# Attention inside a stream of big products: four pieces a tile, or two shared with the neighbour

## The chip, the core and the metric

The kernel runs on one core of one Trainium2 chip. The core has a matrix engine, TensorE (PE in the profile, and PEld for its weight loads), and three others with instruction streams of their own: VectorE (DVE), ScalarE (ACT) and GpSimd (POOL). SyncE (SP) issues the transfers (DMA) between the device memory and the on-chip memory SBUF. PE writes its results to PSUM, eight banks of 512 float32 values for each of 128 partitions, from where DVE and ACT fetch them. The metric is the device time of one execution in microseconds; lower is better.

## The reference

Attention within chunks of 64 tokens, for 4 sequences of 576 tokens and 8 heads of width 64, followed by two feed-forward layers on the 2304 tokens of width 512, each with 2048 hidden units, all in float32:

```python
scores = scale * np.matmul(q_c, k_c.transpose(0, 1, 2, 4, 3))   # 64 x 64 per chunk and head
scores = scores - np.max(scores, axis=-1, keepdims=True)
attn = np.exp(scores)
attn = attn / (np.sum(attn, axis=-1, keepdims=True) + 1e-09)
x = np.matmul(attn, v_c)                                        # then 2304 tokens x 512
h = x @ w_in;  x = (h * sigmoid(1.702 * h)) @ w_out             # first layer
h = x @ w_in;  return (h * tanh(softplus(h))) @ w_out           # second layer, weights of its own
```

## The kernel before

The tokens are cut into 18 tiles of 128 and into NB = 6 blocks of three tiles, 384 tokens. A product of the feed-forward layers is computed to nearly full float32 accuracy from three reduced-precision matmuls: each operand is split into a high part and a low part, and `mm3` (lines 353 to 356) adds high x high, high x low and low x high.

The first layer runs in steps n = 0 to NA - 1 = 95, KF = 16 for each block (the loop at line 748). A step issues `in_proj` (line 358), 12 matmuls of 128 x 384 that give one slice h of 128 hidden units for the block, and, two steps late, `out_a` (line 384), 12 matmuls that add an earlier slice into the block's output, which stays in four banks, acc0 and acc1. Between them, ACT applies the activation (`gelu`, line 370), and DVE splits the result into gh and gl (lines 374 to 380). The slices h take turns in a ring of two banks (tag "h", pool `ps`): a new slice waits until the activation of the one two back has read its bank.

The attention of the next block runs between the steps of the present one, a tile every five steps, in four pieces. Each piece of PE work stands ahead of the `in_proj` of its step:

- step f = 1, 6, 11 of a block: `transposes` (line 253), eight transposes of q and k, which ACT and DVE then copy to SBUF (`take`, line 260);
- the step after: `scores` (line 266), 16 matmuls of 64 x 64 x 64 on quarters of the array; then on DVE the maximum and its subtraction (`shift`), on ACT the exponential, on DVE sums, reciprocal and `normalize`;
- two steps later: `attn_t` (line 311), four transposes of the attention weights, copied by ACT (`take_a`, line 317);
- the step after that: `pv` (line 322), 16 matmuls of 64 x 64 x 64 with v, whose result x is split into a high part by ACT (`x_hi`, line 338) and a low part by DVE (`x_lo`, line 348).

All four pieces of a tile write one PSUM buffer of two banks, tag "at", one after another (`psum`, line 242). The three tiles of the first block come before the loop, in an order that is written out (`PLAN`, line 24), where the buffers of acc0 and acc1 serve as well.

From the second block on, `second.step(n - KF)` (line 489) prepares the second layer's weights at the end of a step, in groups of eight steps (k = 0 to 7): `load` on SP, `scale` on ACT, `join` on DVE, then differences of halves, splits, and stores to device memory. Nothing in the first layer waits for these. The order on every engine is the order of the program: each engine takes its instructions one after another, and the semaphores between them are set when the program is built. The second layer (from line 826) begins after step 95.

Of the kernel before, what the change touches and what calls it, by code (L numbers as in the profile page):

```python
# [16 lines left out]
P = 128  # L17
CH = 64
# [17 lines left out]
def tile_kernel(  # L36
# [193 lines left out]
    class Attention:  # L230
# [16 lines left out]

        def load(self):
            self.q = load_tok(at, "q", q, self.i)
            self.k = load_tok(at, "k", k, self.i)  # L250
            self.v = load_tok(at, "v", v, self.i)

# [12 lines left out]

        def scores(self):
            self.pt = pt = self.psum("sc")
            for u in range(NP // 2):
                for c in range(2):
                    o = (u * 2 + c) * CH  # L270
                    for w in range(2):
                        c0 = (2 * u + w) * P + c * CH
                        for r in range(2):
                            rs = slice(r * CH, (r + 1) * CH)
                            nc.tensor.matmul(  # L275
                                pt[w * CH : (w + 1) * CH, r, o : o + CH],
                                self.qt[rs, c0 : c0 + CH],
                                self.kt[rs, c0 : c0 + CH],
                                start=True,
                                stop=True,  # L280
                            )
# [28 lines left out]

        def attn_t(self):
            self.pt = self.psum("at")
            for p in range(NP):
                s = slice(p * P, (p + 1) * P)
                nc.tensor.transpose(self.pt[:, 0, s], self.e[:, s], ident)  # L315

        def take_a(self, copy):
            if self.a is None:
                self.a = at.tile([P, DM], F32, tag="k", name=f"a{self.i}")
            copy(self.a, self.pt[:, 0, :])  # L320

        def pv(self):
            self.pt = pt = self.psum("pv")
            for p in range(NP):
# [13 lines left out]
        def x_hi(self, copy):  # L338
# [4 lines left out]
            sl = slice(self.t * P, (self.t + 1) * P)  # L343
            self.x = self.pt[:, :, 0 : NP * CH].rearrange("p c (a t) -> p c a t", a=NP)
            self.xo = [x[j][:, :, sl].rearrange("p a (c t) -> p c a t", c=2) for x in (xh, xl)]
# [61 lines left out]
    class Second:  # L407
# [81 lines left out]
        def step(self, s):  # L489
# [14 lines left out]
            if k == 0:  # L504
                self.scale(b)
                self.join(a)
            elif k == 1:
                self.load(c)
                self.join(b)
# [107 lines left out]
    with tc.manual_schedule():  # L617
# [79 lines left out]
        for step in PLAN.split():  # L697
            steps[step[0]](int(step[1:] or 0))
        att = tiles[TT]
        nxt, done, late_lo = tiles[TT + 1], 2, []  # L700

# [46 lines left out]
        for n in range(4, NA):  # L748
            f = n % KF

            if n < NA - KF and f > 0:
                at_step = (f - 1) % 5
                if at_step == 0:
                    att.transposes()
                    att.take("q", act)
                    att.take("k", act if n < KF else vec)
                    if att.i + 1 < NB * TT:
                        nxt = Attention(att.i + 1, usual)
                        nxt.load()
                elif at_step == 1:  # L760
                    att.scores()
                    att.shift()
                    att.exp()
                    att.sums()
                    att.normalize(nc.vector)
                elif at_step == 3:
                    att.attn_t()
                    att.take_a(act)
                elif at_step == 4:
                    att.pv()  # L770
                    att.x_hi(act)
                    att.x_lo()
                    att = nxt

# [329 lines left out]
```

## Time and profile before

| | |
|---|---|
| median of 3 runs | 841.75 us (841.61 to 842.65) |
| the profiled execution | 841.22 us, of which the span of the trace is 839.4 us |
| granted TensorE clock, mean | 0.998 of full speed |
| PE busy | 822.7 us |
| DVE busy | 550.8 us |
| ACT busy | 395.3 us |
| transfers | 180.31 MB, mean 215 GB/s |

Busy time is an average over stages with different limits, so it is read by stage. The first block's attention and its 16 steps take the first 100 us or so, the steps of the other blocks end at about 480 us, and the last attention piece stands at 401 us. PE's matmuls are pipelined: one starts every 0.17 us and is shown for 0.34 us, so what a stretch of PE costs is read from starts, not from busy time. A matmul in float32 on a quarter of the array leaves two records in the trace, so 16 of them are x32.

### The profile page before, as it was taken

What the parts mean: (1) busy time and instruction counts of PE and PEld (TensorE: products, weight loads), DVE (VectorE), ACT (ScalarE), POOL (GpSimd) and SP (SyncE); (2) the same over time, 40 slices, a digit from 0 to 9 for tenths busy, and PEclk for the clock granted to TensorE, in tenths of its full rate; (3) what the DMA queues carried; (4) which work ended last, traced back from release to release, by engine and by line L of the source; (5) the groups of instructions that cost most, each with busy time, mean ns of one, the idle gap of its engine ahead of it and who ended that gap; (6) DMA issues with size and microseconds to landing.
All of it is one profiled execution on the core that took longest, in us unless ns stands there. A gap on an engine that the chain in (4) does not pass through costs nothing.

```text
span 839.4 us, 15656 instructions
## 1 busy us (share of the span) xinstructions
PE 822.7 (98%) x6228; PEld 803.6 (96%) x6228; DVE 550.8 (66%) x1058; ACT 395.3 (47%) x711; POOL 0.7 (0%) x6
## 2 busy tenths in 40 slices
PE   6899999999999999999999999999999999999998
PEld 4799999999999999999999999999999999999997
DVE  6799757657676666766625466688565787565754
ACT  3899644445554544554312443356333465333542
POOL 0000000000000000000000000000000000000000
PEclk9999999999999999999999999999999999999999
DMA  9968635647667673854455178688788787877751
GB/s 242 280 190 246 173 114 150 202 159 242 177 197 212 184 213 138 264 151 164 161 179 226 60 253 322 232 288 261 256 300 282 260 276 260 269 253 240 262 199 57
DMA packets 120135, 180.31 MB, mean 215 GB/s; under 512 B 61440, under 2 KB 82432, under 8 KB 120064
## 3 DMA queue, kind: packets, MB, share of 16 engines
q1 hardware_dynamic: 120064, 179.33, 66.9%
q8 instruction: 49, 0.80, 0.4%
q14 instruction: 22, 0.18, 0.1%
HBM read 140.51 MB, written 38.80 MB: 214 GB/s over the span
## 4 chain that ended last, share of the span: by engine, by line
PE 89%; DVE 5%; ACT 2%; DMA 2%; issue 0%; SPq 0%; DVEq 0%
PE sum_acc L887 16%; PE sum_y L857 12%; PE h L857 9%; PE h L354 7%; PE acc L355 7%; PE acc L356 7%; PE acc L354 7%; PE h L355 7%; PE h L356 7%; PE sum_y L887 6%; DVE raw L201 1%; PE tr L258 1%; DMA raw<-in_moe_w_in_dram 1%; PE sc L275 1%; PE pv L330 1%; PE at L315 1%
## 5 line engine op out<-in xcount | busy, mean ns | idle before, releaser
L354 PE MATMUL h<-xh,wi 128*128 128x384 f32 x384 | 134.9, 351 | 0.0
L356 PE MATMUL h<-xh,wi 128*128 128x384 f32 x384 | 129.1, 336 | 1.7 <-DVE wi L163 1.7
L355 PE MATMUL acc<-gl,wo 128*128 128x384 f32 x384 | 129.2, 337 | 0.7 <-DVE gl L380 0.5
L355 PE MATMUL h<-xl,wi 128*128 128x384 f32 x384 | 129.2, 336 | 0.7 <-DVE xl L350 0.7
L356 PE MATMUL acc<-gh,wo 128*128 128x384 f32 x384 | 129.1, 336 | 0.0
L354 PE MATMUL acc<-gh,wo 128*128 128x384 f32 x384 | 129.0, 336 | 0.0
L372 ACT ACTIVATE t<-h 128x384 f32<-128x384 f32 x96 | 47.0, 489 | 125.4 <-PE h L356 100.0
L376 DVE CAST gh<-t 128x384 fp32r<-128x384 f32 x80 | 28.8, 360 | 90.5 <-ACT t L372 90.4
L354 PEld LDWEIGHTS h<-xh,wi 128*128 128x128 f32 x384 | 72.2, 188 | 2.0
L356 PEld LDWEIGHTS h<-xh,wi 128*128 128x128 f32 x384 | 72.2, 188 | 2.0 <-DVE wi L163 2.0
L355 PEld LDWEIGHTS acc<-gl,wo 128*128 128x128 f32 x384 | 72.2, 188 | 1.3 <-DVE gl L380 1.3
L355 PEld LDWEIGHTS h<-xl,wi 128*128 128x128 f32 x384 | 72.4, 188 | 0.9 <-DVE xl L350 0.9
L356 PEld LDWEIGHTS acc<-gh,wo 128*128 128x128 f32 x384 | 72.2, 188 | 0.0
L354 PEld LDWEIGHTS acc<-gh,wo 128*128 128x128 f32 x384 | 72.2, 188 | 0.0
L380 DVE TENSOR_TENSOR gl<-t,gh 128x384 fp32r<-128x384 f32 x96 | 53.5, 558 | 5.4 <-ACT gh L376 2.7
L867 ACT ACTIVATE v<-h 128x384 f32<-128x384 f32 x24 | 11.9, 494 | 61.9 <-PE h L857 61.9
L926 DVE TENSOR_TENSOR g_a<-u,sum_y 128x384 f32<-128x384 f32 x24 | 13.3, 554 | 32.5 <-PE sum_y L857 32.5
L926 DVE TENSOR_TENSOR v<-u,sum_y 128x384 f32<-128x384 f32 x24 | 13.3, 554 | 30.8 <-PE sum_y L857 30.8
L867 ACT ACTIVATE g_a<-g_a 128x384 f32<-128x384 f32 x24 | 12.6, 526 | 39.0 <-DVE g_a L926 39.0
L867 ACT ACTIVATE v<-v 128x384 f32<-128x384 f32 x24 | 12.6, 524 | 34.4 <-DVE v L926 34.4
L926 DVE TENSOR_TENSOR g_s<-v,g_s 128x384 f32<-128x384 f32 x48 | 26.8, 558 | 0.8
L887 PE MATMUL sum_acc<-fb_p,gh2p 128*128 128x256 f32 x144 | 26.3, 284 | 1.0 <-DVE c L926 1.0
(499 smaller groups left out, 1830.7 us busy)
## 6 DMA issues: line engine op xcount, KB each, us to landing
fs<-w_sums SPq DMA_DIRECT2D x84, 512.0 KB, 4.6
fb_p<-w_out_sums SPq DMA_DIRECT2D x60, 512.0 KB, 4.5
w_sums<-s SPq DMA_DIRECT2D x24, 512.0 KB, 2.7
fa<-w_outs SPq DMA_DIRECT2D x24, 512.0 KB, 4.5
raw<-in_moe_w_in_dram SPq DMA_DIRECT2D x16, 512.0 KB, 5.8
raw<-in_moe_w_out_dram SPq DMA_DIRECT2D x16, 512.0 KB, 4.8
raw2i<-in_moe_w_in_dram SPq DMA_DIRECT2D x16, 512.0 KB, 4.4
raw2o<-in_moe_w_out_dram SPq DMA_DIRECT2D x16, 512.0 KB, 4.9
```

Of the source, the lines that this page charges most:

```text
L201: nc.vector.scalar_tensor_tensor(hi, hi, 3, lo, op0=ALU.logical_shift_left, op1=ALU.bitwise_or)
L258: nc.tensor.transpose(self.pt[:, bank, s], src[:, s], ident)
L354: nc.tensor.matmul(o, wh, mh, start=start, stop=False)
L355: nc.tensor.matmul(o, wh, ml, start=False, stop=False)
L356: nc.tensor.matmul(o, wl, mh, start=False, stop=stop)
L372: nc.scalar.activation(gt[n], hp.pop(n), AF.Gelu_apprx_sigmoid)
L376: (nc.scalar.copy if n < KF else nc.vector.tensor_copy)(gh[n], gt[n])
L380: nc.vector.tensor_tensor(out=gl[n], in0=gt.pop(n), in1=gh[n].bitcast(F32), op=ALU.subtract)
L857: nc.tensor.matmul(h, t[:, u, which, ks], moving[:, kk], start=start and kk == 0 and i == 0, stop=kk == 1 and i == 2, skip_group_check=not ...
L867: nc.scalar.activation(t, c, AF.Mish)
L887: nc.tensor.matmul(o, gs[a][:, ts], w[:, b], start=start and i == 0 and t != 1, stop=stop and i == 2, skip_group_check=again or t > 0,)
L926: nc.vector.tensor_tensor(out=out, in0=x, in1=h, op=op)
```

## The change

From tile 6 on, which is the attention that runs during the second to fifth block's steps, the pieces of neighbouring tiles stand together. In one step come the four transposes of tile i's attention weights and, right behind, the eight transposes of q and k of tile i + 1; in a later step the 16 matmuls of the scores of tile i + 1 and, right behind, the 16 of tile i's product with v. The steps are f = 4, 9, 14 of a block for the transposes and 6, 11, 15 for the others. The four transposes write a bank of the ring "h" instead of the buffer "at", whose two banks the eight then have; scores and pv share one buffer "at", each with half the columns of both banks. The copies and the arithmetic behind each piece stay, but DVE's sums and normalizing move to the start of the following step (`later`), the loads of q and k stand in the step of the transposes, the load of v behind pv, and in the preparation of the second layer `scale(b)` moves from k = 0 to k = 1. The first block's tiles and tiles 3 to 5 keep their four pieces, and so do the scores of tile 6 and pv of tile 17, which have no partner.

```diff
--- before.py
+++ after.py
@@ -246,8 +246,14 @@
             return pool.tile([P, 2, 512], F32, tag=tag, name=f"{what}{self.i}", bufs=1)
 
         def load(self):
+            self.load_qk()
+            self.load_v()
+        def load_qk(self):
             self.q = load_tok(at, "q", q, self.i)
             self.k = load_tok(at, "k", k, self.i)
+        def load_v(self):
             self.v = load_tok(at, "v", v, self.i)
 
         def transposes(self):
@@ -263,8 +269,8 @@
                 setattr(self, f"{which}t", t)
             copy(getattr(self, f"{which}t"), self.pt[:, "qk".index(which), :])
 
-        def scores(self):
-            self.pt = pt = self.psum("sc")
+        def scores(self, pt=None):
+            self.pt = pt = self.psum("sc") if pt is None else pt
             for u in range(NP // 2):
                 for c in range(2):
                     o = (u * 2 + c) * CH
@@ -308,19 +314,19 @@
             rc = self.rc.to_broadcast([P, G, CH])
             eng.tensor_tensor(out=self.eg, in0=self.eg, in1=rc, op=ALU.mult)
 
-        def attn_t(self):
-            self.pt = self.psum("at")
+        def attn_t(self, bank=None):
+            self.pt = self.psum("at")[:, 0, :] if bank is None else bank
             for p in range(NP):
                 s = slice(p * P, (p + 1) * P)
-                nc.tensor.transpose(self.pt[:, 0, s], self.e[:, s], ident)
+                nc.tensor.transpose(self.pt[:, s], self.e[:, s], ident)
 
         def take_a(self, copy):
             if self.a is None:
                 self.a = at.tile([P, DM], F32, tag="k", name=f"a{self.i}")
-            copy(self.a, self.pt[:, 0, :])
-
-        def pv(self):
-            self.pt = pt = self.psum("pv")
+            copy(self.a, self.pt)
+        def pv(self, pt=None):
+            self.pt = pt = self.psum("pv")[:, :, 0 : NP * CH] if pt is None else pt
             for p in range(NP):
                 for c in range(2):
                     cs = slice(c * CH, (c + 1) * CH)
@@ -341,7 +347,7 @@
                 xh[j] = xp.tile([P, KD, TB], F32R, tag=f"xh{j % 2}", name=f"xh{j}")
                 xl[j] = xp.tile([P, KD, TB], F32R, tag=f"xl{j % 2}", name=f"xl{j}")
             sl = slice(self.t * P, (self.t + 1) * P)
-            self.x = self.pt[:, :, 0 : NP * CH].rearrange("p c (a t) -> p c a t", a=NP)
+            self.x = self.pt.rearrange("p c (a t) -> p c a t", a=NP)
             self.xo = [x[j][:, :, sl].rearrange("p a (c t) -> p c a t", c=2) for x in (xh, xl)]
             copy(self.xo[0], self.x)
 
@@ -502,9 +508,9 @@
             if s < 2 or g >= KF // 2:
                 return
             if k == 0:
-                self.scale(b)
                 self.join(a)
             elif k == 1:
+                self.scale(b)
                 self.load(c)
                 self.join(b)
                 self.sum_b("i", g, "t1")
@@ -696,8 +702,21 @@
         a2.a = half_slot("a_first", w1.room("a_first"))
         for step in PLAN.split():
             steps[step[0]](int(step[1:] or 0))
-        att = tiles[TT]
-        nxt, done, late_lo = tiles[TT + 1], 2, []
+        done, late_lo = 2, []
+        later = lambda: None
+        pieces = {("A", 4): 3, ("P", 5): 3}
+        for i in (4, 5):
+            n = 5 * i - 14
+            pieces |= {("T", n): i, ("S", n + 1): i, ("A", n + 3): i, ("P", n + 4): i}
+        pieces |= {("T", KF + 1): 2 * TT, ("S", KF + 2): 2 * TT}
+        for i in range(2 * TT, NB * TT):
+            n, m = (i // TT - 1) * KF, i % TT
+            here = {("A", n + (4, 9, 14)[m]): i, ("P", n + (6, 11, 15)[m]): i}
+            if i + 1 < NB * TT:
+                here |= {(what, at_n): i + 1 for (w, at_n) in here for what in ("T" if w == "A" else "S")}
+            pieces |= here
 
         OUT = ("p5", "p6", "p7", "p3", "p4")
         PLACE = {"p6": 0, "p5": 1, "p7": 2, "p4": 3, "p3": 4}
@@ -748,29 +767,50 @@
         for n in range(4, NA):
             f = n % KF
 
-            if n < NA - KF and f > 0:
-                at_step = (f - 1) % 5
-                if at_step == 0:
-                    att.transposes()
-                    att.take("q", act)
-                    att.take("k", act if n < KF else vec)
-                    if att.i + 1 < NB * TT:
-                        nxt = Attention(att.i + 1, usual)
-                        nxt.load()
-                elif at_step == 1:
-                    att.scores()
-                    att.shift()
-                    att.exp()
-                    att.sums()
-                    att.normalize(nc.vector)
-                elif at_step == 3:
-                    att.attn_t()
-                    att.take_a(act)
-                elif at_step == 4:
-                    att.pv()
-                    att.x_hi(act)
-                    att.x_lo()
-                    att = nxt
+            later()
+            later = lambda: None
+            i_a, i_p, i_t, i_s = (pieces.get((what, n)) for what in "APTS")
+            if i_a is not None:
+                bank = None if i_t is None else ps.tile([P, 512], F32, tag="h", name=f"at{i_a}")
+                tiles[i_a].attn_t(bank)
+                tiles[i_a].take_a(act)
+            if i_t is not None:
+                tiles[i_t].transposes()
+                tiles[i_t].take("q", act)
+                tiles[i_t].take("k", act if n < KF else vec)
+                if i_t + 1 < NB * TT:
+                    tiles[i_t + 1] = Attention(i_t + 1, usual)
+                    tiles[i_t + 1].load_qk()
+                    if i_a is None:
+                        tiles[i_t + 1].load_v()
+            sc = pv = None
+            if i_s is not None and i_p is not None:
+                both = ps_at.tile([P, 2, 512], F32, tag="at", name=f"sp{i_p}", bufs=1)
+                sc, pv = both[:, :, 0 : NP * CH], both[:, :, NP * CH : 2 * NP * CH]
+            if i_s is not None:
+                tiles[i_s].scores(sc)
+            if i_p is not None:
+                tiles[i_p].pv(pv)
+            if i_s is not None:
+                tiles[i_s].shift()
+            if i_p is not None:
+                tiles[i_p].x_hi(act)
+            if i_s is not None:
+                tiles[i_s].exp()
+            if i_p is not None:
+                tiles[i_p].x_lo()
+            if i_s is not None:
+                def later(a=tiles[i_s]):
+                    a.sums()
+                    a.normalize(nc.vector)
+                if n < KF:
+                    later()
+                    later = lambda: None
+            if i_p is not None and i_s is not None and i_p + 2 < NB * TT:
+                tiles[i_p + 2].load_v()
 
             j = n // KF
             hp[n] = in_proj(W[0], (xh[j], xl[j]), f)
```

On PE, in the steps n = 20 to 25 of the second block (at, tr, sc and pv are the buffers of the four pieces, with the tile's number; h4 is the slice of step 20), the order before is:

```order
L315 MATMUL at6_1506<-ident_72,e6_1423 128x128 x4
L354 MATMUL h4_1513<-xh1_684,wi4_532 128x384
...
L330 MATMUL pv6_1553<-a6_1511,v6_1060 64x64 x16
L354 MATMUL h5_1574<-xh1_684,wi5_580 128x384
...
L258 MATMUL tr7_1610<-ident_72,q7_1361 128x128 x4
L258 MATMUL tr7_1610<-ident_72,k7_1363 128x128 x4
L354 MATMUL h6_1629<-xh1_684,wi6_633 128x384
...
L275 MATMUL sc7_1667<-kt7_1621,qt7_1619 64x64 x16
L354 MATMUL h7_1695<-xh1_684,wi7_701 128x384
...
L315 MATMUL at7_1775<-ident_72,e7_1684 128x128 x4
L354 MATMUL h9_1782<-xh1_684,wi9_842 128x384
```

and now it is, with sp6 for the buffer that the scores of tile 7 and pv of tile 6 share:

```order
L321 MATMUL at6_1506<-ident_72,e6_1423 128x128 x4
L264 MATMUL tr7_1513<-ident_72,q7_1361 128x128 x4
L264 MATMUL tr7_1513<-ident_72,k7_1363 128x128 x4
L360 MATMUL h4_1530<-xh1_684,wi4_532 128x384
...
L281 MATMUL sp6_1606<-kt7_1524,qt7_1522 64x64 x16
L336 MATMUL sp6_1606<-a6_1511,v6_1060 64x64 x16
L360 MATMUL h6_1650<-xh1_684,wi6_633 128x384
...
L321 MATMUL at7_1774<-ident_72,e7_1639 128x128 x4
L264 MATMUL tr8_1781<-ident_72,q8_1526 128x128 x4
L264 MATMUL tr8_1781<-ident_72,k8_1528 128x128 x4
L360 MATMUL h9_1798<-xh1_684,wi9_842 128x384
```

The transposes of q and k of tile 7 moved from n = 22 to n = 20, its scores from n = 23 to n = 22, and pv of tile 6 from n = 21 to n = 22.

On DVE, at the end of the third block's attention (step n = 31; xl2 is the low part of x that the products of the third block, n = 32, read; raw2o1 is a weight of the second layer), the order before is:

```order
L461 TENSOR_TENSOR s1_2_2079<-raw2i9_1817,s1_2_2079 128x2x256
L200 TENSOR_SCALAR raw2o1_1931<-raw2o1_1931 128x512
L201 SCALAR_TENSOR_TENSOR raw2o1_1931<-raw2o1_1931 128x512
L350 TENSOR_TENSOR xl2_1571<-pv8_2085,xh2_1570 128x2x4x64
L376 CAST gh31_2119<-t31_2117 128x384
```

and now:

```order
L467 TENSOR_TENSOR s1_2_2094<-raw2i9_1833,s1_2_2094 128x2x256
L200 TENSOR_SCALAR raw2o1_1951<-raw2o1_1951 128x512
L201 SCALAR_TENSOR_TENSOR raw2o1_1951<-raw2o1_1951 128x512
L295 TENSOR_REDUCE mx9_2134<-sp8_2100 128x8
L296 TENSOR_TENSOR e9_2133<-sp8_2100,mx9_2134 128x512
L356 TENSOR_TENSOR xl2_1644<-sp8_2100,xh2_1643 128x2x4x64
L382 CAST gh31_2157<-t31_2155 128x384
```

The maximum and the subtraction for the scores of tile 9 now stand ahead of the low part of tile 8's x, and read the same buffer.

On ACT, in steps n = 50 to 53 (t51 is the activation of step 51, raw2i12 a weight of the second layer, so3 its splits, a12 the copy of transposed attention weights), the order before is:

```order
L372 ACTIVATE t50_3138<-h2_3125 128x384
L460 CAST so3_2_3158<-raw2o11_2843 128x2x256
L460 CAST so3_3_3162<-raw2o11_2843 128x256
L196 ACTIVATE raw2i12_3094<-raw2i12_3094 128x512
L372 ACTIVATE t51_3182<-h3_3169 128x384
L320 COPY a12_3210<-at12_3205 128x512
L372 ACTIVATE t52_3225<-h4_3212 128x384
```

and now:

```order
L378 ACTIVATE t50_3132<-h2_3119 128x384
L466 CAST so3_2_3152<-raw2o11_2838 128x2x256
L466 CAST so3_3_3156<-raw2o11_2838 128x256
L378 ACTIVATE t51_3175<-h3_3162 128x384
L196 ACTIVATE raw2i12_3116<-raw2i12_3116 128x512
L326 COPY a12_3204<-at12_3199 128x512
L270 COPY qt13_3215<-tr13_3206 128x512
L378 ACTIVATE t52_3236<-h4_3223 128x384
```

The scaling of raw2i12 moved behind the activation of step 51, and the copies for tile 12 and tile 13 now stand side by side.

## Rows read from the trace of the kernel before

**Rows 1.** The page, part 1: busy us, share of the span, instructions.

```profile
PE 822.7 (98%) x6228; PEld 803.6 (96%) x6228; DVE 550.8 (66%) x1058; ACT 395.3 (47%) x711; POOL 0.7 (0%) x6
```

**Rows 2.** Waits of PE, whole span: waited for, us in total, times, longest.

```profile
PE at L315 <- DVE e L309: 5.7, 2, 4.7
```

**Rows 3.** Busy time by stretch: stretch, its us, then each engine's busy us.

```profile
100.00:402.00 302.00, 302.00 (x2450) 293.58 (x2449) 201.68 (x417) 143.56 (x239) 0.00 (x0) 1.00 0.60 182
```

**Rows 4.** Timeline of PE around a pv piece: start, us, engine, line, operation.

```profile
124.74 0.34 PE L356 MATMUL acc<-gh,wo 128*128 128x384 f32 x1
...
126.30 0.34 PE L356 MATMUL acc<-gh,wo 128*128 128x384 f32 x1
126.56 0.69 PE L330 MATMUL pv<-a,v 64*64 64x64 f32 x32
...
127.47 0.34 PE L355 MATMUL h<-xl,wi 128*128 128x384 f32 x1
```

**Rows 5.** Timeline of PE around a scores piece.

```profile
136.33 0.34 PE L356 MATMUL acc<-gh,wo 128*128 128x384 f32 x1
...
137.50 0.34 PE L355 MATMUL h<-xl,wi 128*128 128x384 f32 x1
```

**Rows 6.** The same scores piece, the timeline begun inside it, at two places.

```profile
136.71 0.59 PE L275 MATMUL sc<-kt,qt 64*64 64x64 f32 x28
...
137.06 0.24 PE L275 MATMUL sc<-kt,qt 64*64 64x64 f32 x4
```

**Rows 7.** Timeline of PE around eight transposes, then around four.

```profile
131.28 0.34 PE L356 MATMUL acc<-gh,wo 128*128 128x384 f32 x1
131.46 0.60 PE L258 MATMUL tr<-ident,q 128*128 128x128 f32 x4
...
132.51 0.34 PE L355 MATMUL h<-xl,wi 128*128 128x384 f32 x1
...
145.48 0.34 PE L356 MATMUL acc<-gh,wo 128*128 128x384 f32 x1
145.65 0.60 PE L315 MATMUL at<-ident,e 128*128 128x128 f32 x4
...
146.26 0.34 PE L355 MATMUL h<-xl,wi 128*128 128x384 f32 x1
```

**Rows 8.** Timeline of PE's weight loads at the way into the scores.

```profile
136.60 0.56 PEld L275 LDWEIGHTS sc<-kt,qt 64*64 64x64 f32 x32 [0.25 <-issue]
```

**Rows 9.** Timeline at the end of the third block's attention, DVE, ACT, PE.

```profile
174.84 0.69 DVE L201 SCALAR_TENSOR_TENSOR raw2o<-raw2o 128x512 int32<-128x512 int32 x1
174.88 0.59 ACT L346 CAST xh<-pv 128x512 fp32r<-128x512 f32 x1 [1.14 <-PE pv L330]
175.50 0.69 DVE L350 TENSOR_TENSOR xl<-pv,xh 128x512 fp32r<-128x512 f32 x1
...
179.19 0.34 PE L355 MATMUL h<-xl,wi 128*128 128x384 f32 x1
```

**Rows 10.** Timeline of DVE behind the scores of a tile.

```profile
137.93 0.68 DVE L289 TENSOR_REDUCE mx<-sc 128x8 f32<-128x512 f32 x1
138.65 0.69 DVE L290 TENSOR_TENSOR e<-sc,mx 128x512 f32<-128x512 f32 x1
```

**Rows 11.** Timeline of ACT and PE between steps 51 and 52.

```profile
272.70 0.69 ACT L196 ACTIVATE raw2i<-raw2i 128x512 f32<-128x512 f32 x1 [1.22 <-DMA raw2i<-in_moe_w_in_dram]
...
273.23 0.42 PE L354 MATMUL h<-xh,wi 128*128 128x384 f32 x1
273.28 0.48 ACT L372 ACTIVATE t<-h 128x384 f32<-128x384 f32 x1
```

**Rows 12.** Waits of all engines, 100 to 402 us.

```profile
DVE kt L264 <- ACT qt L264: 8.5, 10, 2.1
...
ACT s L460 <- DMA w_sums<-s: 7.9, 5, 2.1
```

**Rows 13.** The page, part 6: DMA issues, KB each, us to landing.

```profile
raw2o<-in_moe_w_out_dram SPq DMA_DIRECT2D x16, 512.0 KB, 4.9
```

## The prediction

> **What bounds the kernel now.** I read the busy table first: the reader is to see that PE is busy for 98% of the span [rows 1]. Then the list of waits on PE: it is short, its longest entry is 5.7 us in two waits of the start-up [rows 2], and asked for 100 to 402 us alone, where the work that the change touches runs, it has no entry at all. The table by stretch says the same from the other side: 302.00 us of PE work in 302.00 us [rows 3]. So in this stretch nothing that DVE, ACT or a DMA does is waited for, and the time can only change by what PE itself takes for its stream, or by a wait that does not exist yet. Last I read the stream of PE around the pieces of attention, for what a piece costs beyond its own matmuls.
>
> **The stream.** In the big products a matmul starts every 0.173 us: nine steps from 124.74 to 126.30 are 1.56 us [rows 4]. Around a pv piece the step from the last big matmul to the second one behind it (the first start behind a piece is early, the second is back in the rhythm) is 127.47 - 126.30 = 1.17 us; without the piece it would be 2 x 0.173 = 0.347. A pv piece costs 0.823 us. For the scores 137.50 - 136.33 = 1.17 gives 0.823 again [rows 5]. Both pieces hold 16 matmuls on a quarter of the array, which leave 32 records. Inside a run they go fast: with 28 records left it is 136.71, with 4 left 137.06, so 24 records take 0.35 us, 14.6 ns each [rows 6], and 32 take 0.467. The other 0.823 - 0.467 = 0.356 us is the border: getting in from the big products and out to them. At the way in the weight load starts only when the matmul does, at 136.60, after 0.25 us without one [rows 8]; in the big stream it runs ahead under the matmul before. For the transposes the same subtraction gives 146.26 - 145.48 - 0.347 = 0.433 us for four and 132.51 - 131.28 - 0.347 = 0.883 us for eight [rows 7]: 0.108 and 0.110 each, so there is no border to speak of.
>
> **The change, part by part.** The same instructions run; only their order, their PSUM place and the waits change. From tile 6 on, the order of PE shows 11 pairs of scores and pv standing together and 11 triples of transposes standing together; tile 6's scores and tile 17's pv stay alone.
>
> Scores with pv: apart 2 x 0.823 = 1.646 us, together 0.356 + 2 x 0.467 = 1.290. Each pair saves 0.356, eleven save 3.92 us, all on the path, since PE is the path. No row of before shows a pv matmul right behind a score, so this has two ends: if the seam is one more step of 58 ns per four records, as inside either run, the saving is whole; if the seam costs a border of its own, it is nothing. I take the whole: inside a run each matmul already brings its own weights and goes to another quarter of the array than the one before, and the seam asks for no more.
>
> Here the page "TensorEngine Tiling (Array Packing)" of the Trainium skill, section Tiling Modes (Key Properties), has a rule: changing the tiling mode drains TensorE, changing only the tile does not. The rows agree as far as they go, with 0.356 us at a change of mode and 14.6 ns inside; by the rule the seam is free and the sum whole, and were the border due to new operands instead, the second rival below would hold.
>
> Transposes together: apart 0.433 + 0.883 = 1.316, together twelve at 0.108 to 0.1125 (the last is what four more cost, 0.450) are 1.30 to 1.35. Eleven of them are -0.4 to +0.2 us; I take 0, the two rows being alike per transpose.
>
> The h bank: the attention transposes now use a buffer of the ring of two that the first-layer products use. So the products of that step wait for the gelu of the step before, where until now they waited for the one before that. The tightest place is step 51: its gelu ran from 273.28 for 0.48 us, since ACT in front of it had waited for a weight and scaled it (272.70), and the products of step 52 started at 273.23 [rows 11]. They will start one run of eight transposes later, 0.88 us, at 274.11, against a gelu that is done at 273.76: 0.35 us to spare. And the scaling in front of that gelu moves behind it, which gives back 0.69 us and its wait. Cost 0; the cover is this slack.
>
> One PSUM tile for scores and pv: DVE's maximum and subtraction of the scores now start behind pv (0.467 us later), the copy of x on ACT behind DVE's reads, and x's low part behind that copy. What waits for it is the next block's products, at three block borders. At the one at 174 us DVE was busy with a weight until 174.84 + 0.69 = 175.53, x's high part ran from 174.88, the low part from 175.50 to 176.19, and PE read it at 179.19 [rows 9]. Now DVE from 175.53: 0.68 + 0.69 for the scores [rows 10], 0.59 on ACT, 0.69 on DVE, and about 0.1 of hand-over each time, is 178.4; PE reads at 179.19 + 0.47 = 179.66. The slack falls from 3.0 to 1.3 us and covers it. Cost 0.
>
> That the readers must go one behind another is a rule of the page "PSUM — Partial Sum Buffer" of the Trainium skill (PSUM bank collisions): two engines must not touch a bank's quadrant at once. This trace has the order already, DVE's copy of k waiting for ACT's copy of q, 8.5 us in ten waits [rows 12]. Were they side by side, the low part would end 1.4 us sooner and the sum would be the same.
>
> The rest: sums and normalizing go to the next step's start; their reader, the transposes, comes three steps after the scores or later, over 12 us. The scaling of a weight moves one step on, into the step of its join on DVE: there gelu and scaling stand before it on ACT, gh and gl on DVE, so a wait is short, and DVE feeds nothing there that PE reads within a step. On SP the q and k loads now stand ahead of some weight loads and wait for the transposes of their own step; the v loads wait for pv. The weight loads held behind them are read two steps later, 2 x 24 x 0.173 = 8.3 us, and land in 4.9 [rows 13]. Cost 0 each.
>
> Sum: 3.9 us off the profiled execution's 841.22, 837.3. The median of the runs, 841.75, lies 0.53 above that execution, so the median to come is 837.8.
>
> **Rivals.** (1) The seam between scores and pv is a border too, in part or whole, for instance since pv's first matmul carries a wait of its own. For it: no row shows the seam. Against: the matmuls on both sides are of one form. Half a border gives 839.8, a whole one 841.7. (2) The slack at the block borders or in the h bank is not enough here and there, since ACT and DVE get their work in another order. For it: 1.3 us and 0.35 us are not much. Against: the lateness of step 51 came from what is moved away. If three places lose 1 us each, 840.8. (3) The slower side: the h bank as the new bound. If at all eleven steps the gelu comes as late as at step 51 and behind one more wait of ACT for a store, 2.1 us at its longest [rows 12], PE stands 2.1 - 0.35 = 1.75 us at each, 19.3 in all, and the time is 841.75 - 3.9 + 19.3 = 857.1. It decides from 0.36 us per place on, where it has eaten the saving. Against: in most steps the gelu waits for nothing but its products.
>
> **How the numbers follow.** My forecast, the whole saving and no wait, 76%: 837.8, by itself 837.0 to 838.6, the width of the three runs of before and the ±0.4 of the transposes. Rival 1 10%, rival 2 10%, rival 3 4%. What a measurement of this kernel can tell from no change is about 0.2%, 1.7 us: faster means below 840.1. The forecast and a good half of rivals 1 and 2 lie there, 0.87; the rest of them within, 0.09; rival 3 slower, 0.04. The range leaves out rival 3, the worse part of the other two and a little at the low end: 837.0 to 840.8.
>
> **What would show it.** In the profile after: 64 records of the quarter-array in one row of PE, with about 1.64 us from the last big matmul to the second behind it, against 1.17 for 32; a second start gap in the middle of that row would be rival 1. The row of twelve transposes should take 1.66 by the same measure. The list of PE's waits must stay empty between the first block and 400 us: an entry of h waiting for gelu would be the h bank, one of h waiting for xl the block border. The first matmul of the second layer should come about 3.9 us sooner, and nothing after it should give that back. I am wrong if that start moves by less than 2 us.

## The result and the profile after

The kernel became slower. Five runs of each: 851.08 us (850.40 to 852.63) against 842.10 (841.61 to 842.65), a ratio of 1.0105 with an interval of 1.0095 to 1.0116. The forecast was 837.8 us, in a range that ended at 840.8. The profiled execution took 852.63 us, of which the span is 850.9. One of the four executions of experiment e3 took 1626.59 us, about twice as long as the other three, and is left out of its figures below.

First the page's busy times, then the stretch of the shared work by time (same columns as [rows 1] and [rows 3]):

```profile
PE 824.1 (97%) x6228; PEld 804.4 (95%) x6228; DVE 547.2 (64%) x1058; ACT 395.0 (46%) x711; POOL 0.7 (0%) x6
```
```profile
110.00:412.00 302.00, 292.33 (x2370) 283.82 (x2367) 192.53 (x406) 139.85 (x233) 0.00 (x0) 1.00 0.58 178
```

The engines do the same work as before, but PE, which filled this stretch to the last microsecond [rows 3], now stands still for 9.67 us in it. The granted clock is 1.00, as it was. The waits of PE over the whole span, which had one long entry [rows 2]:

```profile
PE at L321 <- DVE e L315: 6.5, 4, 4.8
PE sp L281 <- DVE kt L270: 5.4, 3, 1.8
PE h L360 <- ACT t L378: 2.3, 3, 1.4
...
PE acc L361 <- DVE gl L386: 1.7, 1, 1.7
...
PE pv L336 <- ACT a L326: 0.9, 1, 0.9
```

The entries for `kt`, `t` and `a` are new: every one is a wait for something that ACT computes or copies, or that DVE copies behind ACT. (The 1.7 us for `gl` lie before 110 us, at the end of the first block; the same entry is 0.5 us before, and between 0.5 and 2.3 us in the kernels below, with and without a loss.)

Yet the saving is there. A shared step is a step in which scores and product with v stand together; a triple is the three groups of four transposes in one step. PE around the first shared piece, from the last big matmul to the second one behind (answering to [rows 4, 5]), and around the first full triple of transposes (answering to [rows 7]):

```profile
133.67 0.34 PE L362 MATMUL acc<-gh,wo 128*128 128x384 f32 x1
133.94 0.69 PE L281 MATMUL sp<-kt,qt 64*64 64x64 f32 x32
134.46 0.65 PE L336 MATMUL sp<-a,v 64*64 64x64 f32 x32
...
135.31 0.34 PE L361 MATMUL h<-xl,wi 128*128 128x384 f32 x1
...
147.45 0.34 PE L362 MATMUL acc<-gh,wo 128*128 128x384 f32 x1
147.62 0.60 PE L321 MATMUL at<-ident,e 128*128 128x128 f32 x4
...
148.49 0.60 PE L264 MATMUL tr<-ident,k 128*128 128x128 f32 x4
...
149.11 0.34 PE L361 MATMUL h<-xl,wi 128*128 128x384 f32 x1
```

The pair takes 135.31 - 133.67 = 1.64 us, 1.293 without the 0.347 of two big steps; the prediction had 1.290. The second run starts 0.52 us behind the first, 0.05 more than 32 records of 14.6 ns: the seam is no border. The triple takes 1.66, the 1.66 forecast. In e3 below, where nothing stands, all eleven pairs take 1.64 or 1.65 us and all eleven triples 1.66.

So something takes far more than the saving. From tile 6's first transposes to tile 17's product with v, the same place in PE's stream in both, it was 107.68 to 400.62 us, 292.94; now it is 110.02 to 412.02, 302.00. That is 9.06 us more, as much as the medians differ (9.0); the rest of the span behind it is as long as before (438.8 us). The two profiled executions differ by more, 11.5 us of span: the other 2.3 lie ahead of tile 6's transposes, a place that was reached at 107.7 to 111.0 us in the kernels below, with a loss and without one, so that they look like scatter of the start. Without the 4 us saved it is 13 us of standing. Compared gap by gap with a kernel that has the same pieces and doesn't stand (experiment e3), these 13 are: three shared pieces that wait for `kt`, 5.6; five slices h (`in_proj`) that wait for a gelu, 3.6; five triples that wait for the normalized `e`, 1.7; three products into the block's output (`out_a`), 1.2; the last product with v, 1.0. (The list of waits shows less, since PE counts as busy for some 0.2 us behind each last matmul.)

**Where they begin.** ACT at a scores step of before, with the end of DVE's shift at 138.65 + 0.69 = 139.34 [rows 10]; an `ACT_TABLE_LOAD` is the change from gelu's table to exp's, or back:

```profile
136.24 1.28 ACT L298 ACT_TABLE_LOAD   x1
139.38 0.63 ACT L298 ACTIVATE e<-e 128x512 f32<-128x512 f32 x1 [1.85 <-DVE e L290]
140.02 1.28 ACT L372 ACT_TABLE_LOAD   x1
141.32 0.49 ACT L372 ACTIVATE t<-h 128x384 f32<-128x384 f32 x1
```

The first load runs while ACT would wait for DVE anyway. After, DVE's shift and ACT at the first shared step:

```profile
135.90 0.69 DVE L296 TENSOR_TENSOR e<-sp,mx 128x512 f32<-128x512 f32 x1
...
136.66 0.59 ACT L352 CAST xh<-sp 128x512 fp32r<-128x512 f32 x1 [2.31 <-DVE e L296]
137.27 1.28 ACT L304 ACT_TABLE_LOAD   x1
138.56 0.63 ACT L304 ACTIVATE e<-e 128x512 f32<-128x512 f32 x1
139.21 1.28 ACT L378 ACT_TABLE_LOAD   x1
140.51 0.49 ACT L378 ACTIVATE t<-h 128x384 f32<-128x384 f32 x1
```

In the shared step `x_hi` (L352) stands ahead of `exp` on ACT, and it reads the tile that DVE reads: now it is the one that waits for DVE, and the table load stands behind it and is exposed. The step's gelu starts 140.51 - 136.59 = 3.92 us behind the end of DVE's shift; before, 141.32 - 139.34 = 1.98.

The page "ScalarE: Activation LUTs" of the Trainium skill, section What ACT_TABLE_LOAD costs, gives 1283 ns for the load and about 1380 ns of drain more at each switch. The load agrees, 1.28 us in each row; the drain is not to be seen: the load at 139.21 starts 0.02 us behind the exp.

**How it reaches PE.** Some steps later in the third block, timeline of ACT, DVE, SP and PE:

```profile
162.02 0.69 DVE L296 TENSOR_TENSOR e<-sp,mx 128x512 f32<-128x512 f32 x1
...
166.94 0.49 ACT L378 ACTIVATE t<-h 128x384 f32<-128x384 f32 x1
...
167.46 0.36 DVE L382 CAST gh<-t 128x384 fp32r<-128x384 f32 x1 [3.06 <-ACT t L378]
...
168.25 0.67 ACT L466 CAST s<-raw2i 128x512 fp32r<-128x512 f32 x1
...
173.56 0.68 DVE L467 TENSOR_TENSOR s<-raw2i,s 128x512 fp32r<-128x512 f32 x1
...
174.28 4.45 SPq L469 DMA_DIRECT2D w_sums<-s  x2
...
177.00 0.65 ACT L466 CAST s<-raw2i 128x512 fp32r<-128x512 f32 x1 [6.04 <-DMA w_sums<-s]
177.55 0.58 ACT L326 COPY a<-at 128x512 f32<-128x512 f32 x1
178.03 0.59 ACT L270 COPY qt<-tr 128x512 f32<-128x512 f32 x1
...
178.65 0.69 DVE L270 COPY kt<-tr 128x512 f32<-128x512 f32 x1 [0.28 <-ACT qt L270]
...
179.40 0.69 PE L281 MATMUL sp<-kt,qt 64*64 64x64 f32 x32 [1.81 <-DVE kt L270]
```

The weights of the second layer go through a chain that lies on two in-order engines and a queue: split on ACT (L466, the cast into `s`), joined on DVE, stored by SP; the next split can only start when the store has landed and freed its slot in a ring of five (NRAW), which the weights share. Nothing in the first layer reads these weights, but what stands behind them in a queue waits with them. The gelu is late, so the split behind it is; DVE waits 3.06 us for the gelu ahead of its part; the store starts late; and the next split waits 6.04 us for it, at the head of ACT's queue. Behind it stand the copies of `a` and `qt`, and behind these the scores. Tiles 9, 12 and 15 have their transposes one step before their scores (steps 14 and 15 of a block), the others two, and at these three places PE stands 1.8 us. ACT's waits for stores at a split in the stretch (`s` and `so`), and for DVE at `x_hi`:

```profile
ACT s L466 <- DMA w_sums<-s: 33.1, 8, 6.0
ACT xh L352 <- DVE e L296: 30.4, 11, 3.2
...
ACT so L466 <- DMA w_out_sums<-so: 23.3, 7, 4.2
```

Before, the wait at `s` was 7.9 us in five [rows 12], and that at `so` 4.2 us in five.

### The profile page after: what moved, and what is told of

Same layout as the page of the kernel before. It is cut to its first block, busy times and chain, and to the rows that moved or that the text cites. A ratio compares the mean times of both kernels' runs of the same rounds, so it can differ in the third digit from the quotient of the medians.

```text
span 850.9 us, 15669 instructions
## 1 busy us (share of the span) xinstructions
PE 824.1 (97%) x6228; PEld 804.4 (95%) x6228; DVE 547.2 (64%) x1058; ACT 395.0 (46%) x711; POOL 0.7 (0%) x6
## 3 DMA queue, kind: packets, MB, share of 16 engines
HBM read 140.51 MB, written 38.80 MB: 211 GB/s over the span
## 4 chain that ended last, share of the span: by engine, by line
PE 63%; DVE 17%; ACT 8%; DMA 8%; issue 3%; SPq 0%; ACTq 0%; DVEq 0%
PE sum_acc L927 15%; PE sum_y L897 12%; PE h L897 9%; PE sum_y L927 6%; DMA w_out_sums<-so 4%; PE acc L361 3%; PE h L360 3%; PE acc L360 3%; PE acc L362 3%; PE h L362 3%; PE h L361 3%; DMA w_sums<-s 3%; ACT L378 2%; ACT L304 2%; DVE gl L386 2%
## 5 line engine op out<-in xcount | busy, mean ns | idle before, releaser
L466 ACT CAST so<-raw2o 128x256 fp32r<-128x256 f32 (+1 forms) x40 | 20.7, 523 | 44.5 <-DMA w_out_sums<-so 23.3
L466 ACT CAST s<-raw2i 128x512 fp32r<-128x512 f32 (+1 forms) x32 | 19.2, 600 | 35.1 <-DMA w_sums<-s 33.7
L467 DVE TENSOR_TENSOR so<-raw2o,so 128x256 fp32r<-128x256 f32 (+1 forms) x40 | 20.3, 527 | 21.4 <-ACT so L466 21.4
L467 DVE TENSOR_TENSOR s<-raw2i,s 128x512 fp32r<-128x512 f32 (+1 forms) x32 | 19.9, 622 | 21.8 <-ACT s L466 21.8
```

Source lines behind the costliest of these rows:

```text
L466: nc.scalar.copy(hi, w)
L467: nc.vector.tensor_tensor(out=lo, in0=w, in1=hi.bitcast(F32), op=ALU.subtract)
```

## The experiments

Lines with - are the changed kernel's, unless another is named; "PE idle" is of 110 to 410 us (8.79 in the changed kernel). The kernel before took 842.93 (e1 to e4), 842.56 (e5 to e8) and 842.90 us (e9 to e12) on the same chips.

**e1: scores and product with v in steps of their own again, transposes together.**

```diff
-            here = {("A", n + (4, 9, 14)[m]): i, ("P", n + (6, 11, 15)[m]): i}
+            here = {("A", n + (4, 9, 14)[m]): i, ("P", n + (5, 10, 15)[m]): i}
...
-                here |= {(what, at_n): i + 1 for (w, at_n) in here for what in ("T" if w == "A" else "S")}
+                here |= {("T", n + (4, 9, 14)[m]): i + 1, ("S", n + (6, 11, 16)[m]): i + 1}
...
-            if i_p is not None and i_s is not None and i_p + 2 < NB * TT:
+            if i_p is not None and i_p >= 2 * TT and i_p + 2 < NB * TT:
```

> The changed kernel with scores and pv apart again (pv at steps 5, 10, 15, scores at 6, 11, 16), the transposes still together and in the ring's bank. Theory A (the shared tile: x's high part on ACT waits for DVE's two reads of the scores, the load of the exponential's table comes only behind it, the gelu of that step is late, DVE and the splits of the second layer's weights slip, ACT stands in front of stores): PE's waits between 110 and 412 us, 9.7 us in the changed kernel, fall under 2 us, and with the saving of 3.9 gone the time is 842 to 844. Rival B (the h bank holds PE): the waits stay above 5 us, 848 to 853. Rival C (the third tile's transposes only one step ahead of its scores, three waits of 1.9 us): 5.6 us of waits go, since the scores come two steps later here, 848 or so.

Measured: 841.92 us, ratio 0.9995 [0.9984, 1.0005], PE idle 0. With the transposes together on the bank of `h`, no wait comes up: the bank alone isn't the cause. It gains nothing either, as the 0 for the transposes said. The loss needs the shared step (e1 also sets the third tile's scores two steps behind its transposes; e3 below leaves them at one and loses nothing).

**e2: the reverse, transposes apart, on a buffer of their own, scores with the product with v** (in place of the lines that e1 changes):

```diff
+            here = {("A", n + (4, 9, 13)[m]): i, ("P", n + (6, 11, 15)[m]): i}
...
+                here |= {("T", n + (5, 10, 14)[m]): i + 1, ("S", n + (6, 11, 15)[m]): i + 1}
...
-                    if i_a is None:
+                    if i_t <= 2 * TT:
```

> The changed kernel with the attention weights' transposes (steps 4, 9, 13) apart from those of q and k (5, 10, 14) and in the at buffer, so the ring h is the products' alone; scores and pv still together. Theory A: the waits stay, above 6 us, and the time is 847 to 852. Rival B (the h bank): they go, the saving of 3.9 us is left, 838 to 840. Rival C (spacing): all tiles now have one step between transposes and scores, so it is no better than the changed kernel, 850 or more.

Measured: 853.86, ratio 1.0132 [1.0115, 1.0149], PE idle 9.05. A loss is there without the bank, at another place, and above theory A's range; its list of PE's waits from 110 to 412 us is one line:

```profile
PE at L321 <- DVE e L315: 9.0, 4, 2.4
```

None is for `kt`, as rival C's spacing would have it. The gelu is as late as in the changed kernel (3.92 us or more behind the shift), but at these four places it reaches PE by another way, without the stores: DVE waits for the gelu at `gh` (3.05 us at 164.33), the sums and the normalizing of `e` stand behind it on DVE, and the transposes of `e` come only two steps behind the scores here (13 and 11 of a block, 14 and 11 in the changed kernel); PE waits 2.40 us for `e` at 168.79. ACT's waits for these stores are down to 7.0 and 12.1 us. So e2 shows that a late gelu costs time without the bank, but not by the chain above.

**e3: in the shared step, exp ahead of x_hi.**

```diff
-            if i_p is not None:
-                tiles[i_p].x_hi(act)
             if i_s is not None:
                 tiles[i_s].exp()
             if i_p is not None:
+                tiles[i_p].x_hi(act)
                 tiles[i_p].x_lo()
```

> The changed kernel with the exponential ahead of x's high part on ACT in the shared steps, so that the table can load while ACT waits for DVE. Theory A: the gelu of these steps comes 1.3 us sooner, a good part of the waits goes, 843 to 848. Rivals B, C and D (the scaling of a weight moved by a step): no change, 850 to 852.

Measured: 837.95 (837.89 to 839.05, three executions), ratio 0.9947 [0.9931, 0.9964], PE idle 0. That is better than theory A expected: not a good part of the waits went, but all of them. The place of the stall above in this kernel, then the stretch:

```profile
156.54 1.28 ACT L304 ACT_TABLE_LOAD   x1
159.40 0.63 ACT L304 ACTIVATE e<-e 128x512 f32<-128x512 f32 x1 [1.58 <-DVE e L296]
159.94 0.57 ACT L352 CAST xh<-sp 128x512 fp32r<-128x512 f32 x1
160.53 1.28 ACT L378 ACT_TABLE_LOAD   x1
161.82 0.49 ACT L378 ACTIVATE t<-h 128x384 f32<-128x384 f32 x1
...
171.87 0.66 ACT L466 CAST s<-raw2i 128x512 fp32r<-128x512 f32 x1 [3.20 <-DMA w_sums<-s]
```
```profile
110.00:412.00 302.00, 302.00 (x2470) 297.46 (x2470) 204.17 (x429) 143.60 (x244) 0.00 (x0) 1.00 0.59 184
```

The load is back under the wait; gelu starts 2.45 us behind DVE's shift (which ends at 159.37), not the 4.23 of this place after; the split waits 3.20 us, not 6.04, and PE not at all. In the changed kernel the gelu was 1.78 us later than here; PE stood 0.9 us at products and transposes soon after, and 1.81 us at the scores some steps on. From tile 6's transposes to tile 17's product with v it is 108.42 to 397.28 us, 288.86: 4.08 less than before. That is the prediction's 3.92, whole.

**e4: the scaling of a weight back in its old step.**

```diff
             if k == 0:
+                self.scale(b)
                 self.join(a)
             elif k == 1:
-                self.scale(b)
                 self.load(c)
```

> The changed kernel with the scaling of weight b back in the step before its join (k = 0). Rival D (the moved scaling makes DVE wait in its join and shifts the splits): most waits go, 840 to 844. Theory A and rivals B and C: within 1.5 us of the changed kernel, 850 to 852.

Measured: 852.35, ratio 1.0114 [1.0099, 1.0130], PE idle 8.37. The scaling's step is of no account.

**e5: order as in the changed kernel, but exp's table called for ahead of x_hi,** by an exp of one column of a constant:

```diff
+            if i_s is not None and i_p is not None:
+                early = st.tile([P, 1], F32, tag="early", name=f"early{i_s}")
+                nc.scalar.activation(early, ident[:, 0:1], AF.Exp)
             if i_p is not None:
                 tiles[i_p].x_hi(act)
```

> The changed kernel with x's high part still ahead of the exponential, and a one-column exponential of a constant put ahead of both in the shared steps, so that the table loads while ACT waits for DVE. Theory A1 (the 1.28 us of the table load, no longer under a wait, are what makes the step too long): the waits of PE between 110 and 410 us vanish as with the exponential first, 838 to 840. Theory A2 (the exponential and the gelu stand 0.6 us behind the copy of x, and DVE's order with them): 848 to 852. If both have a share: 841 to 847.

Measured: 838.98, ratio 0.9953 [0.9938, 0.9968], PE idle 0. ACT in the same step:

```profile
157.06 1.28 ACT L799 ACT_TABLE_LOAD   x1
...
159.99 0.59 ACT L352 CAST xh<-sp 128x512 fp32r<-128x512 f32 x1 [1.43 <-DVE e L296]
160.47 0.64 ACT L304 ACTIVATE e<-e 128x512 f32<-128x512 f32 x1
```

The order of the two is kept, an instruction is added, and the loss is gone: it is the load's place, not that x_hi goes first or that exp goes last.

**e6: in shared steps, the split of gelu's output on DVE behind the second-layer weights' work,** so that DVE doesn't wait at it.

```diff
-            g_hi(n)
+            behind = i_s is not None and i_p is not None
+            if not behind:
+                g_hi(n)
...
+                if behind:
+                    g_hi(n)
+                    g_lo(n)
```

> The changed kernel with gh and gl of the shared steps behind the second layer's DVE work of that step, so that DVE does not stand at gh until the late gelu is done. Theory M1 (the lateness reaches the splits through DVE's queue): most waits of PE go, 838 to 843. Theory M2 (it goes through ACT's own queue, whose casts stand behind the gelu): little change, 848 to 852.

Measured: 855.53, ratio 1.0150 [1.0132, 1.0168], PE idle 11.35, more than either theory expected. It freed nothing: PE's waits for `kt` are still 5.5 us in three, and waits for `gh` and `gl` came on top, which the edit itself brings, since it makes these later. That DVE's standing at `gh` isn't by itself what holds the chain is likely from the waits for `kt`, but not shown cleanly.

**e7: a sixth raw slot for the weights' chain** (room taken from the ring of gelu's outputs, 5 to 4, and from a constant that only the start-up uses), the order untouched.

```diff
-NRAW = 5
+NRAW = 6
...
-    gp = ctx.enter_context(tc.tile_pool(name="gp", bufs=5))
+    gp = ctx.enter_context(tc.tile_pool(name="gp", bufs=4))
...
-        zeros = const.tile([P, TB], BF16, name="zeros")
+        zeros = tmp.tile([P, TB], F32, tag="t", name="zeros").bitcast(BF16)[:, 0:TB]
```

> The changed kernel with six raw slots in place of five (four buffers for gh and gl in place of five, and the start-up's zeros in a buffer of t, to make room). Theory R (the splits of the second layer's weights wait for one spare slot and hold ACT in front of the attention's copies): ACT's waits for stores, 58 us between 109 and 412 in the changed kernel, fall under 25 and PE's waits there under 3 us, 839 to 844. Rival (the long chain of the shared step itself makes PE wait): waits of PE above 6 us, 847 to 852.

Measured: 837.77, ratio 0.9939 [0.9924, 0.9954], PE idle 0; theory R expected less, 839 to 844. ACT in the same steps:

```profile
159.01 1.28 ACT L304 ACT_TABLE_LOAD   x1
160.31 0.63 ACT L304 ACTIVATE e<-e 128x512 f32<-128x512 f32 x1
...
168.33 0.68 ACT L466 CAST s<-raw2i 128x512 fp32r<-128x512 f32 x1
169.75 0.59 ACT L326 COPY a<-at 128x512 f32<-128x512 f32 x1 [0.74 <-PE at L321]
```

The load is as exposed as in the changed kernel (1.28 us with ACT waiting for nothing), and the gelus come 3.92 us behind the shift, but the split at 168.33 waits for no store, and ahead of the copy of `a` it is ACT that waits for PE, 0.74 us. So in this schedule there are two links, and either one cut is enough: the exposed load, and the chain with one slot to spare that hands it on.

**e8: the kernel before, with a one-column copy of DVE's result on ACT ahead of exp from tile 7 on,** which exposes the load in the old, four-piece schedule.

```diff
+                    if att.i > 2 * TT:
+                        seen = st.tile([P, 1], F32, tag="seen", name=f"seen{att.i}")
+                        nc.scalar.copy(seen, att.e[:, 0:1])
                     att.exp()
```

> The kernel before, with a copy of one column of the shifted scores on ACT ahead of the exponential from tile 7 on, so that ACT waits for DVE first and loads the table after. If the exposed table load alone is enough: PE waits appear between 107 and 402 us and the time is 844 to 852. If it hurts only together with the longer shared step: 842 to 843.5, no entry in the list of PE's waits there.

Measured: 843.48, ratio 1.0009 [0.9999, 1.0018], PE idle 0. The gelu comes 3.48 us behind the shift there, not 1.98, in eleven steps, and that cost nothing that could be told from none. So the old schedule had room for an exposed load. That shared steps have less, since they carry x_hi on ACT and their scores end later, is likely but was not tested by itself.

**e9 and e10: how much room.** From e3, one or two copies of `e` onto itself on ACT behind x_hi in each shared step, 0.6 us each.

```diff
+                if i_s is not None:
+                    for _ in range(1):
+                        act(tiles[i_s].e, tiles[i_s].e)
```

> The version with the exponential first, and behind x's high part of the shared steps one copy of the shifted scores onto themselves on ACT, some 0.6 us a step ahead of the second table load and the gelu. If time on ACT ahead of the gelu is what counts, and the shared step has a little room: 838 to 840, hardly any waits of PE. If there is no room at all, half of the loss is back: 843 to 847.

> The same with two such copies, 1.2 us a step, about the table load of the changed kernel. If time on ACT ahead of the gelu is what counts, whatever fills it: the loss comes back, 847 to 853, with waits of PE for kt and gelu between 110 and 410 us. If it was the table load itself, or the order of exponential and copy: 838 to 841.

Measured: 842.98, 0.9998 [0.9986, 1.0009], PE idle 2.14; and 847.21, 1.0057 [1.0043, 1.0071], PE idle 6.13. From tile 6's transposes to tile 17's product with v they took 291.75 and 296.87 us, 2.9 and 8.0 more than e3. e10's first shared step, then its waits of PE from 110 to 412 us:

```profile
137.11 1.27 ACT L802 COPY e<-e 128x512 f32<-128x512 f32 x2
138.40 1.28 ACT L378 ACT_TABLE_LOAD   x1
139.70 0.49 ACT L378 ACTIVATE t<-h 128x384 f32<-128x384 f32 x1
```
```profile
PE sp L281 <- DVE kt L270: 5.0, 3, 1.9
PE pv L336 <- ACT a L326: 0.5, 1, 0.5
PE at L321 <- DVE e L315: 0.3, 1, 0.3
```

The same three places, with exp's load under the wait again. Put beside each other by how long behind DVE's shift the gelu starts in the first shared step: 2.45 us (e3, run again as e11) gives 838.5, 2.96 (e9) gives 843.0, 3.63 (e10) gives 847.2, and the changed kernel's 3.92 gives 851.1. In shared steps it is any time on ACT ahead of the gelu that counts, and the room ends somewhere between 2.45 and 2.96 us. Past 2.45, a microsecond in each of the eleven steps costs about 7 to 9 by the medians and 6 to 9 by the stretch (13.1 us in the changed kernel). The scale holds for shared steps with five slots alone: in e8 3.48 us cost nothing, in e7 3.92.

**e11 and e12: the cures again, in five rounds,** e3 alone and e3 with e7's sixth slot.

> The version with the exponential first once more, for a narrow interval: 837.8 to 839, that is 0.994 to 0.996 of the kernel before.

> Exponential first and six raw slots together. Neither version has a wait of PE between 110 and 410 us, so nothing is left to gain there: within 0.7 us of the exponential first alone, 837.3 to 838.7. If the six slots or the four buffers for gh and gl do something elsewhere, outside that.

Measured: 838.48 (837.94 to 839.94), 0.9957 [0.9945, 0.9970]; and 838.06 (837.61 to 838.13), 0.9947 [0.9933, 0.9961]. Both beat the kernel before and the changed one; one from the other can't be told. With the order mended the sixth slot brings nothing to be seen. What the slot would do in the kernel before was not run.

## Why the prediction was wrong, point by point

- **What bounds the kernel**: right. PE is the bound, and the time changed by its own stream and by a wait that did not exist before. The prediction named both ways and priced only one of them rightly.
- **Scores with pv, 3.92 us**: right in mechanism and size. 1.293 us a pair against 1.290; 4.08 us between the same two points where nothing stands (e3). The seam is free, and rival 1 falls; this agrees with the rule on tiling modes that the prediction took from the Trainium skill ("TensorEngine Tiling (Array Packing)", Tiling Modes).
- **Transposes together, 0**: right (1.66 us for twelve, e1 at 0.9995).
- **The h bank, 0**: the cover of 0.35 us held where the gelus were in time (e1, no wait). After, five products did wait for a gelu, 3.6 us in all, but because the gelus were late for another reason: with the bank kept and the gelu in time (e3) there is none. Rival 3, which had the slower side by this wait at 857.1, is so refuted as the cause, though its sign came true.
- **One PSUM tile for scores and pv, 0**: this is the step that failed; in place of 0 it cost, with what follows from it, 13.1 us (302.00 against e3's 288.86). It followed what waits for x's low part, found the block borders, and there it was right: no product of a next block waits for `xl` in the stretch. It priced "the copy of x on ACT behind DVE's reads" only for those who wait for x. It did not ask what is queued behind that copy on ACT: exp's table load, which had run under the wait for DVE, then exp, gelu's load and the gelu. 1.94 us more between shift and gelu (3.92 - 1.98), 1.28 of it the load. And rows 12 had a sign for the rest: ACT already waited five times for a store at a split, up to 2.1 us, so that a chain through a store stood at times at the head of the queue that carries the copies of `a` and `qt`. That was used for rival 3 alone. It is no more than a sign: with the same ring, the kernel before bore gelus 1.5 us later (e8). The row that the prediction sets beside the rule of the Trainium skill ("PSUM — Partial Sum Buffer", PSUM bank collisions), DVE's copy of k behind ACT's copy of q, is of two readers of one tile in two different banks, so it shows an order by tile and not by bank; and the low part of x could not have run beside the high part, which it reads.
- **The rest, 0**: held. The scaling's step is of no account (e4), and the late q and k loads nobody waited for.
- **Rival 2** (slack not enough here and there, "since ACT and DVE get their work in another order") named the kind of cause, with a tenth of the chance and three places at 1 us. It was three places at 1.8 us and some fourteen smaller ones, 13 us in all: the bound of it should have come from ACT's queue, not from the slack at the block borders.

What stays open: why the room on ACT ends between 2.45 and 2.96 us. That the ring with one spare slot hands the lateness on is shown (e7); which of its links is the tightest isn't, and e6, which brought waits of its own, doesn't settle it.

## What to carry to other kernels

Where two pieces are put into one step, write down every in-order queue of that step, old and new, and ask of each instruction that now waits what stands behind it; a table load was free here only where it stood ahead of the wait and not behind it. An engine that is busy for less than half of the time can still have no room at all, if a chain with one spare buffer passes through its queue: waits for a store in the profile before are a reason to look, though not a proof, since the kernel before had them and still had room (e8). Before giving up a change that lost time, compare the bound engine's stream gap by gap: here the saving was whole, and swapping two calls brought it out.

## What the runs showed of the hardware that was not expected

- A change of ACT's table costs 1.28 us in the row, at every one of its places, and the next instruction follows 0.01 to 0.02 us behind where its operand is there; the load is issued without waiting for the operand of the activation that needs it (156.54 in e3, 1.58 us of waiting behind it).
- 64 records on the quarter-array in one run cost the way in and out only once: 0.52 us from the first start of one half to that of the other, though they write to different columns of one tile and read different operands.
- ACT and DVE each took their turn on the shared tile in every one of the eleven steps, though ACT reads other columns than DVE's shift: ACT's copy starts 0.08 to 0.38 us behind the end of the shift in the changed kernel. (DVE's low part, 0.03 us behind ACT's copy, reads that copy and would have to wait for it anyway.) The order is that of the program's semaphores; what the two engines would do without it no run shows.
